# First forward stage on sums and differences of mirrored rows, in 32x32 tiles of TensorE

## The chip, the cores and the metric

The kernel runs on one core of one Trainium2 chip. A core has five engines that run side by side and wait for each other by semaphores: TensorE (PE in the profile; PEld is its loading of weights), VectorE (DVE), ScalarE (ACT), GpSimd (POOL) and SyncE (SP), which here only issues DMA transfers. Matmuls write to PSUM, eight banks of 128 partitions by 512 fp32; VectorE or ScalarE carry ("evict") the results to SBUF. The metric is the device time of one execution in microseconds, the median of three runs.

## The reference

```python
X = np.fft.rfft(x, axis=1)                      # x: 8 x 3008 x 256
Y = X * (filt_r + 1j * filt_i)[None]            # filter of 1505 x 256
y = np.fft.irfft(Y, n=3008, axis=1)
h = y.reshape(24064, 256) @ w_in                # 256 x 2048
g = 0.5 * h * (1.0 + erf(h / sqrt(2)))
out = g @ w_out                                 # 2048 x 256
```

Each of 8 batches is mixed along its 3008 rows by a Fourier transform, a filter and the transform back. Then comes a feed-forward layer with a GELU over all 24064 rows.

## The kernel before

The transform is factored as 3008 = 47 x 64. Row n of a batch is n = 64 * n1 + n2. **Stage 1** transforms over the 47 values of n1 for each n2; as x is real, frequencies k = 0..23 are enough, a real part (a sum of x times cosines) and an imaginary part (times sines), 48 rows in all. Its result R1 goes through DRAM, to be read back in another order (**r1**). **Stage 2** transforms over n2 and multiplies by the filter, **stage 3** goes back over n2, and its result R2 also goes through DRAM (**r2**); **stage 4** goes back over n1 and writes a ring `y_sb`. The feed-forward layer works on tiles of 512 rows: `mm1` makes 128 of the 2048 hidden columns, ScalarE applies the GELU, `mm2` multiplies by `w_out`.

Batch 0 is mixed first, in a form of its own (functions c1 to c4). The main loop then goes through slots, sixteen to a tile. In each slot are one step of `mm1` for tile t and one of `mm2` for tile t-1. The stages of batches 1 to 7 are spread over these slots, ahead of the tiles that need them.

```python
    for b in range(1, B):
        hi = first(b)                 # first slot that needs batch b
        if b == 1:
            s1, n1, r1, s2, n2, r2, s4, n4 = 0, 4, 15, 25, 2.8, 61, 68, 0.72
        else:
            s1, n1, r1, s2, n2, r2, s4, n4 = hi - 94, 3.5, hi - 80, hi - 69, 3.5, hi - 24, hi - 17, 1
        for u in range(16):
            put(s4 + int(u * n4), m.s4, b, u // 2, u % 2)
        for c in range(4):
            put(s1 + int(c * n1), m.s1, b, c)
            put(r1, m.r1, b, c)
            put(r2, m.r2, b, c)
        # ... s2, s3, and the loads of the next batch's x, behind gates on s2's results
    for s in range((NT + 1) * 16):
        t, jc = s // 16, s % 16
        for f, a in at.pop(s, ()):
            f(*a)
        if t >= 1:
            m.mm2(t - 1, jc)
        if t < NT:
            m.mm1(t, jc)
```

In the first sixteen slots there is no tile t-1, so only `mm1` and its GELU run there, beside stage 1 of batch 1.

Stage 1 works on four chunks of 16 columns of n2 (8 in each half). `x_sb` holds the 47 rows of n1 on 94 or, from batch 1 on, 111 of 128 partitions: columns n2 < 32 from partition 0, the others from partition 64. One matmul multiplies 47 rows by a 47x48 matrix, padded to 64 columns, on a quarter of TensorE's array:

```python
    def s1(self, b, c):
        # ...
        a = self.pa.tile([128, 2, 4, 256], BF16, tag="a", name="a_sb")
        x = self.st[b, "x"]
        ps = [[self.bank("ps_s1", "h" if i == h == 0 else "f") for h in range(2)] for i in range(2)]
        for i in range(2):
            for r in range(2):
                for h in range(2):
                    w = 8 * c + 4 * r + 2 * i
                    nc.tensor.matmul(ps[i][h][64 * r:64 * r + 64, :], lhsT=self.T1s[64 * h:64 * h + NA],
                                     rhs=x[64 * h:64 * h + NA, w:w + 2, :], start=True, stop=True)
        for i in range(2):
            for h in range(2):
                self._evac(a[:, h, 2 * i:2 * i + 2, :].rearrange("p a b -> p (a b)"), ps[i][h], False)
        o = self.st[b, "R1"].rearrange("n q c -> q n c")
        for r in range(2):
            for h in range(2):
                w = HB * h + 8 * c + 4 * r
                nc.sync.dma_start(out=o[:, w:w + 4, :], in_=a[64 * r:64 * r + 48, h])
```

`_evac(..., False)` is a copy on VectorE, `"act"` one on ScalarE. In PSUM three banks belong to tag `h` (used by `mm1` too), two to `o` (`mm2`) and three to `f`.

Before the main loop GpSimd makes the matrix and issues the loads of batch 1, eight transfers of 47 rows, and then those of `w_out`:

```python
    m.table_1_tiles(g)
    m.load_x(1)
    m.load_w_out(0)
    m.load_w_out(8)
    m.weights_4(g)
```

Of the kernel before, what the change touches and what calls it, by code (L numbers as in the profile page):

```python
# [10 lines left out]
ALU = mybir.AluOpType  # L11
FP32 = mybir.dt.float32
BF16 = mybir.dt.bfloat16
I32 = mybir.dt.int32
# [3 lines left out]
NA, NB = 47, 64  # L18
K1 = 24
HB = 32  # L20
# [9 lines left out]
class _Mix:  # L30
    def __init__(self, ctx, tc, x, filt_r, filt_i, w_in, w_out, out):
        self.tc, self.nc = tc, tc.nc
        self.x, self.filt_r, self.filt_i = x, filt_r, filt_i
        self.w_in, self.w_out, self.out = w_in, w_out, out
        self.B, self.S, self.D = x.shape
        self.DFF = w_in.shape[1]
        assert self.S == NA * NB and self.D == 256 and self.DFF == 2048
        pool = lambda name, bufs, **kw: ctx.enter_context(tc.tile_pool(name=name, bufs=bufs, **kw))
        P = bass.MemoryType.PSUM
        self.const = pool("const", 1)  # L40
        self.px = pool("px", 2)
        self.pa = pool("pa", 3)
        self.pb = pool("pb", 4)
        self.pp = pool("pp", 4)
        self.pv = pool("pv", 3)
        self.pd = pool("pd", 4)
        self.pool = pool
        self.po = pool("po", 3)
        self.py = pool("py", 1)
        self.pg = pool("pg", 2)  # L50
        self.small = pool("small", 1)
        self.dram = pool("dram", 2, space=bass.MemoryType.DRAM)
        c = self.const
# [21 lines left out]
    def load_x(self, b, lo=0, n=32, hs=(0, 1)):  # L75
        nc = self.nc
        if lo == 0 and 0 in hs:
            self.st[b, "x"] = self.px.tile([128 if b else 2 * NA, HB, 256], BF16, tag="x", name="x_sb")
        xt, o = self.st[b, "x"], 64 if b else NA
        xv = self.x[b].rearrange("(n1 h w) d -> h n1 w d", h=2, w=HB)  # L80
        for w in range(lo, lo + n, 8):
            for h in hs:
                nc.gpsimd.dma_start(out=xt[h * o:h * o + NA, w:w + 8, :], in_=xv[h][:, w:w + 8, :])  # L83

    def load_filters(self, k0, k):

        nc, D = self.nc, self.D
        for t, src in enumerate((self.filt_r, self.filt_i)):
            direct = _dram(src, k0 * D, [[NA * D, 32], [D, k], [1, D]])
            mirror = _dram(src, (NA - k0) * D, [[NA * D, 32], [-D, k], [1, D]])  # L90
            for q, a in enumerate((direct, mirror)):
                nc.gpsimd.dma_start(out=self.F[32 * q:32 * q + 32, t, k0:k0 + k, :], in_=a)
# [11 lines left out]
    def load_next(self, b, p, c, h):  # L104

        self.gate(self.st[b, "p", p][0:1, 0:1])
        self.load_x(b + 1, 8 * c, 8, (h,))

    def load_w_in(self):
        wi = self.w_in.rearrange("(dc p) j -> p dc j", p=128)  # L110
# [14 lines left out]
    def table_1(self, g):  # L125

        nc, ts = self.nc, self.nc.vector.tensor_scalar
        col = lambda name: g.tile([128, 1], FP32, name=name)
        off = g.tile([128, 2, K1], FP32, name="off")
# [12 lines left out]
        nc.vector.tensor_tensor(out=w, in0=w, in1=r, op=ALU.subtract)  # L142
        for q, s in enumerate((hc, hs)):
            nc.scalar.activation(out=self.T1[:, 48 * q:48 * q + 48], in_=w[0:2 * NA].rearrange("p a b -> p (a b)"),
                                 func=AF.Sin, scale=s[0:2 * NA])
# [131 lines left out]
            self.nc.vector.tensor_scalar(out=out, in0=in_, scalar1=scale, scalar2=None, op0=ALU.mult)  # L277


    def table_1_tiles(self, g):  # L280

        v = self.nc.gpsimd
        self.T1s = g.tile([128, 64], BF16, name="T1s")
        v.memset(self.T1s, 0.0)
        for r in (0, 64):
            v.tensor_copy(out=self.T1s[r:r + NA, 0:48], in_=self.T1[0:NA, 0:48])

    def s1(self, b, c):

        nc = self.nc  # L290
        if c == 0:
            self.st[b, "R1"] = self.dram.tile([NB, 48, 256], BF16, tag="R1", name="R1")
        a = self.pa.tile([128, 2, 4, 256], BF16, tag="a", name="a_sb")
        x = self.st[b, "x"]
        ps = [[self.bank("ps_s1", "h" if i == h == 0 else "f") for h in range(2)] for i in range(2)]
        for i in range(2):
            for r in range(2):
                for h in range(2):
                    w = 8 * c + 4 * r + 2 * i
                    nc.tensor.matmul(ps[i][h][64 * r:64 * r + 64, :], lhsT=self.T1s[64 * h:64 * h + NA],  # L300
                                     rhs=x[64 * h:64 * h + NA, w:w + 2, :], start=True, stop=True)
        for i in range(2):
            for h in range(2):
                self._evac(a[:, h, 2 * i:2 * i + 2, :].rearrange("p a b -> p (a b)"), ps[i][h], False)
        o = self.st[b, "R1"].rearrange("n q c -> q n c")
        for r in range(2):
            for h in range(2):
                w = HB * h + 8 * c + 4 * r
                nc.sync.dma_start(out=o[:, w:w + 4, :], in_=a[64 * r:64 * r + 48, h])

    def r1(self, b, c):
        bt = self.pb.tile([128, 6, 256], BF16, tag="b", name="b_sb")
# [219 lines left out]
def kernel(  # L532
# [9 lines left out]
    m = _Mix(ctx, tc, x, filt_r, filt_i, moe_w_in, moe_w_out, out)  # L542
    nc, B, S = tc.nc, m.B, m.S
# [89 lines left out]
    m.warm_up(2)  # L633
    m.T1p = g.tile([2 * NA, 2, K1, 2], BF16, name="T1p")
    nc.gpsimd.tensor_copy(out=m.T1p, in_=m.T1.rearrange("p (h r k) -> p h k r", h=2, r=2))
    m.table_1_tiles(g)
    m.load_x(1)
    m.load_w_out(0)
    m.load_w_out(8)
    m.weights_4(g)  # L640

    warm = g.tile([128, 1], FP32, name="warm")
# [12 lines left out]
    def put(slot, f, *a):  # L655
        at.setdefault(slot, []).append((f, a))

    def first(b):
        return (b * S // TCH) * 16

    for b in range(1, B):
        hi = first(b)
        if b == 1:
            s1, n1, r1, s2, n2, r2, s4, n4 = 0, 4, 15, 25, 2.8, 61, 68, 0.72
        else:
            s1, n1, r1, s2, n2, r2, s4, n4 = hi - 94, 3.5, hi - 80, hi - 69, 3.5, hi - 24, hi - 17, 1
# [9 lines left out]
        if b + 1 < B:  # L676
            for i in range(8):
                put(s2 + int(n2 * (i + 2)), m.load_next, b, i + 2, i // 2, i % 2)
# [41 lines left out]
```

## Time and profile before

The time is 772.04 us, the median of three runs between 771.49 and 772.39. The profiled execution took 771.8.

| Item (page of the profile) | Count | Mean ns | Busy us |
|---|---|---|---|
| stage 1 matmuls, 512 columns (L300) | 224 | 389 | 18.3 |
| their evictions on VectorE (L275, a_sb) | 112 | 683 | 69.5 |
| output evictions on VectorE (L519, ost) | 93 | 687 | 63.9 |
| GELU on ScalarE (L489) | 752 | 597 | 437.9 |
| mm1 matmuls (L486) | 1600 | 366 | 445.9 |
| mm2 matmuls (L513) | 2992 | 273 | 447.7 |

The profile is of one execution. A line of its groups has the line of the kernel, the engine, the operation, what it writes and reads with the shapes, the count; after the first bar the busy time in microseconds and the mean of one in nanoseconds, after the second the idle time of the engine just before, and what ended it. Busy times are unions: matmuls overlap in the array, so their means say more of latency than of cost, and the cost of a stage on TensorE is better read from when it and its neighbours start. The chain of waits goes back from the last instruction, at each step to what released it. A line of the timeline has the start and the length in microseconds, the engine, the line and the operation.

### The profile page before, as it was taken

The numbers are of one execution on the slowest core, as the hardware profiler recorded it, in microseconds if no ns is written. First come the engines' busy times: TensorE is split into PE (matmuls) and PEld (weight loads), VectorE is DVE, ScalarE is ACT, GpSimd is POOL, SyncE is SP. The second block draws the span as 40 slices with busy tenths as digits, with TensorE's granted clock in tenths as the row PEclk, the third lists the DMA queues.
The fourth block names the chain that finished last, engine by engine and source line by source line (L and its number), as shares of the span: only waits on it lengthen the run. The fifth ranks groups of instructions, "written<-read, shape, count | busy, mean of one in ns | idle before, by whom it ended". The sixth has DMA issues, their size and how long they took to land.

```text
span 771.8 us, 15047 instructions
## 1 busy us (share of the span) xinstructions
PE 763.0 (99%) x6057; PEld 527.2 (68%) x6057; DVE 399.0 (52%) x735; ACT 567.8 (74%) x978; POOL 63.7 (8%) x157
## 2 busy tenths in 40 slices
PE   8999999999999999999999999999999999999998
PEld 4757675676776766667677767666776776766666
DVE  8966755464545645457463664637646366411011
ACT  7879855897568975699656996579865798666663
POOL 8701100010000200011000110001100000000000
PEclk9999999999999999999999999999999999999999
DMA  9795645466153661636516465355553422410111
GB/s 151 130 191 130 146 113 125 130 128 150 54 147 102 136 162 41 191 77 124 142 54 181 85 133 123 81 152 97 122 137 82 138 83 69 123 42 28 42 42 55
DMA packets 87270, 85.66 MB, mean 111 GB/s; under 512 B 6688, under 2 KB 77472, under 8 KB 87200
## 3 DMA queue, kind: packets, MB, share of 16 engines
q1 hardware_dynamic: 78816, 68.70, 31.6%
q0 software_dynamic: 8384, 16.00, 14.7%
q8 instruction: 47, 0.77, 0.4%
q14 instruction: 23, 0.19, 0.1%
HBM read 54.00 MB, written 46.66 MB: 130 GB/s over the span
## 4 chain that ended last, share of the span: by engine, by line
PE 97%; DMA 1%; DVE 1%; POOL 0%; issue 0%; SPq 0%; DVEq 0%; POOLq 0%
PE ps_o L513 42%; PE ps_h L486 42%; PE ps_s L373 2%; PE ps_s L348 2%; PE ps_s L323 2%; PE ps_s L300 2%; DMA x_sb<-in_x_dram 1%; PE ps_c L434 1%; PE ps_c3t L449 0%; PE ps_c L412 0%; DMA d_sb<-R 0%; PE ps_warm L267 0%; POOL x_sb L83 0%; PE ps_c L463 0%; DVE T3i L260 0%; PE ps_c1t L399 0%
## 5 line engine op out<-in xcount | busy, mean ns | idle before, releaser
L489 ACT ACTIVATE g_sb<-ps_h 128x512 bf16<-128x512 f32 x752 | 437.9, 597 | 182.7 <-PE ps_h L486 172.0
L513 PE MATMUL ps_o<-w_out_sb,g_sb 128*128 128x256 bf16 x2992 | 447.7, 273 | 0.0
L486 PE MATMUL ps_h<-y_sb,w_in_sb 128*128 128x512 bf16 (+3 forms) x1600 | 445.9, 366 | 0.3 <-DVE a_sb L275 0.3
L513 PEld LDWEIGHTS <-g_sb 128*128 128x128 bf16 x2992 | 283.8, 98 | 134.3 <-issue 9.9
L486 PEld LDWEIGHTS <-w_in_sb 128*128 128x128 bf16 x1600 | 154.8, 98 | 23.7 <-issue 1.3
L519 DVE COPY ost<-ps_o 128x512 f32<-128x512 f32 x93 | 63.9, 687 | 143.7 <-PE ps_o L513 143.6
L331 DVE TENSOR_TENSOR p<-ps_s,F 128x512 bf16<-128x512 f32 x84 | 58.1, 692 | 105.2 <-ACT p L330 89.1
L277 DVE TENSOR_SCALAR y_sb<-ps_s 128x376 bf16<-128x376 f32 x112 | 61.0, 548 | 80.7 <-PE ps_s L373 80.7
L275 DVE CAST a_sb<-ps_s 128x512 bf16<-128x512 f32 x112 | 69.5, 683 | 27.5 <-PE ps_s L300 26.5
L275 DVE CAST v_sb<-ps_s 128x512 bf16<-128x512 f32 x84 | 57.4, 685 | 2.9 <-PE ps_s L348 2.9
L329 ACT ACTIVATE p<-ps_s 64x512 bf16<-64x512 f32 x84 | 49.8, 593 | 2.1
L330 ACT CAST p<-ps_s 64x512 bf16<-64x512 f32 x84 | 48.5, 577 | 1.0
L373 PEld LDWEIGHTS <-d_sb 96*128 96x128 bf16 x448 | 30.8, 97 | 25.6 <-DMA d_sb<-R 0.6
L102 POOL COPY gate<-p 1x1 bf16<-1x1 bf16 x48 | 8.5, 176 | 469.0 <-DVE p L333 469.0
L333 DVE TENSOR_TENSOR p<-p 128x512 bf16<-128x512 bf16 x84 | 35.7, 425 | 2.9
L373 PE MATMUL ps_s<-T,d_sb 96*128 96x94 bf16 x448 | 36.3, 204 | 0.1
L332 DVE TENSOR_TENSOR p<-p,F 128x512 bf16<-128x512 bf16 x84 | 34.9, 416 | 0.0
L83 POOL DMA_DIRECT2D x_sb<-in_x_dram x64 | 32.9, 516 | 13.3 <-issue 12.2
L323 PE MATMUL ps_s<-b_sb,T 128*128 128x256 bf16 x168 | 32.1, 273 | 0.0
L348 PE MATMUL ps_s<-p,T 128*128 128x256 bf16 x168 | 32.1, 273 | 0.0
L348 PEld LDWEIGHTS <-T 128*128 128x128 bf16 x168 | 16.4, 98 | 19.8 <-DVE p L333 0.4
L323 PEld LDWEIGHTS <-T 128*128 128x128 bf16 x168 | 16.4, 98 | 13.4
(114 smaller groups left out, 196.1 us busy)
## 6 DMA issues: line engine op xcount, KB each, us to landing
out_dram<-ost SPq DMA_DIRECT2D x93, 256.0 KB, 2.5
x_sb<-in_x_dram POOLq DMA_DIRECT2D x64, 188.0 KB, 3.8
R<-a_sb SPq DMA_DIRECT2D x112, 96.0 KB, 2.1
b_sb<-R SPq DMA_DIRECT2D x28, 384.0 KB, 4.2
R<-v_sb SPq DMA_DIRECT2D x42, 256.0 KB, 3.5
d_sb<-R SPq DMA_DIRECT2D x56, 192.0 KB, 4.9
w_in_sb<-in_moe_w_in_dram POOLq DMA_DIRECT2D x2, 512.0 KB, 10.6
w_out_sb<-in_moe_w_out_dram POOLq DMA_DIRECT2D x2, 512.0 KB, 11.9
```

The lines of the kernel that those rows point to most:

```text
L275: self.nc.vector.tensor_copy(out=out, in_=in_)
L277: self.nc.vector.tensor_scalar(out=out, in0=in_, scalar1=scale, scalar2=None, op0=ALU.mult)
L323: nc.tensor.matmul(ps[:, 256 * i:256 * i + 256], lhsT=self.T2[:, k].rearrange("p a b -> p (a b)"), rhs=self.st[b, "b", k // 6][:, k % 6, : ...
L329: nc.scalar.activation(out=p2[0:64], in_=ps[64:128], func=AF.Copy, scale=-1.0)
L330: nc.scalar.copy(out=p2[64:128], in_=ps[0:64])
L331: nc.vector.tensor_tensor(out=p1, in0=ps, in1=f(0), op=ALU.mult)
L348: nc.tensor.matmul(ps[:, 256 * i:256 * i + 256], lhsT=self.T3[:, k].rearrange("p a b -> p (a b)"), rhs=w[:, 256 * i:256 * i + 256], start= ...
L373: nc.tensor.matmul(ps[:, 94 * i:94 * i + 94], lhsT=d[:, (grp % 2) * 4 + i, 128 * half:128 * half + 128], rhs=t4, start=True, stop=True)
L486: nc.tensor.matmul(ps[:, o:o + n], lhsT=self.w_in_sb[:, dc, jc * 128:jc * 128 + 128], rhs=self.ring[:, dc, off:off + n], start=(dc == 0), ...
L489: nc.scalar.activation(out=self.st["g", t][:, jc, :], in_=ps, func=AF.Gelu)
L513: nc.tensor.matmul(ps[:, tile_i % 2, :], lhsT=g[:, jc, tile_i * 128:tile_i * 128 + 128], rhs=self.w_out_sb[:, jc, :], start=(jc == 0), sto ...
L519: nc.vector.tensor_copy(out=ost, in_=ps)
```

## The change

The 47 rows of n1 pair up: row m and row 47-m have the same cosine and opposite sines. So the real part needs only the 24 sums x[m] + x[47-m], and the imaginary part only the differences, each times a 24x24 matrix instead of a 47x48. (Row 0 is its own partner: it is added to itself, and its matrix row is halved.) The change makes sums and differences on VectorE ("fold"), a batch ahead for three of four chunks, and puts the small matrices on all sixteen 32x32 tiles of the array. It is for TensorE, which should stream half as many columns for stage 1. `[...]` marks cuts.

```diff
+        self.pf = pool("pf", 3)
-        self.pv = pool("pv", 3)
+        self.pv = pool("pv", 2)
-        self.po = pool("po", 3)
+        self.po = pool("po", 2)
[...]
+    def load_pairs(self, b, c):
+        if c == 0:
+            self.st[b, "x"] = self.px.tile([128, 2, 4, 1024], BF16, tag="x", name="x_sb")
+        t = self.st[b, "x"]
+        rows = self.x.rearrange("b (n e) d -> (b n) (e d)", e=4)
+        for i in range(2):
+            self.nc.gpsimd.indirect_dma_start(
+                out=t[:, i, c], out_offset=None, in_=rows, element_offset=(b * self.S // 4 + c) * 1024,
+                in_offset=bass.IndirectOffsetOnAxis(ap=self.rows_at[i], axis=0))
[...]
+    def load_next(self, b, p, c):
         self.gate(self.st[b, "p", p][0:1, 0:1])
-        self.load_x(b + 1, 8 * c, 8, (h,))
+        self.load_pairs(b + 2, c)
+    def load_second(self, c):
+        self.gate(self.st[1, "b", c][0:1, 0, 0:1])
+        self.load_pairs(2, c)
[...]
+    def row_indices(self, g):              # twelve iotas: rows m and 47-m, in four groups of 32 partitions
[...]
+    def table_1_pairs(self, g):            # on GpSimd: the 0/1 matrix "pick" that selects rows of T1
[...]
+    def table_1_rows(self):
+        ps = self.bank("ps_t1", "n")
+        self.nc.tensor.matmul(ps[:, 0:48], lhsT=self.pick[0:2 * NA], rhs=self.T1[:, 0:48], start=True, stop=True)
+        self._evac(self.T1s[:, :, 0:K1], ps[:, 0:48].rearrange("p (r k) -> p r k", r=2), "act")
+
+    def fold(self, b, c):
+        x = self.st[b, "x"]
+        s = self.st[b, "fold", c] = self.pf.tile([128, 4, 256], BF16, tag="xs", name="xs")
+        d, m, s = x[:, 0, c], x[:, 1, c], s.rearrange("p a b -> p (a b)")
+        self.nc.vector.tensor_tensor(out=s, in0=d, in1=m, op=ALU.add)
+        self.nc.vector.tensor_tensor(out=d, in0=d, in1=m, op=ALU.subtract)
 
     def s1(self, b, c):
[...]
+        rows = (self.st.pop((b, "fold", c)), self.st[b, "x"][:, 0, c].rearrange("p (a b) -> p a b", a=4))
+        ps = [self.bank("ps_s1", "f" if g else "h") for g in range(4)]
+        for j in range(2):
             for r in range(2):
-                for h in range(2):
-                    w = 8 * c + 4 * r + 2 * i
-                    nc.tensor.matmul(ps[i][h][64 * r:64 * r + 64, :], lhsT=self.T1s[64 * h:64 * h + NA],
-                                     rhs=x[64 * h:64 * h + NA, w:w + 2, :], start=True, stop=True)
+                for g in range(4):
+                    o, w, k = 64 * j + 32 * r, 2 * j, slice(32 * g, 32 * g + K1)
+                    nc.tensor.matmul(ps[g][o:o + 32, :], lhsT=self.T1s[k, r, :],
+                                     rhs=rows[r][k, w:w + 2, :].rearrange("p a b -> p (a b)"), start=True, stop=True)
+        for g in range(4):
+            self._evac(a[:, g].rearrange("p a b -> p (a b)"), ps[g], "act" if g == 3 or b == 1 and g == 1 else False)
+        o = self.st[b, "R1"].rearrange("(g w) (r k) c -> r w k g c", g=4, r=2)
+        for j in range(2):
+            for r in range(2):
+                for i in range(2):
+                    p = 64 * j + 32 * r
+                    nc.sync.dma_start(out=o[r, 4 * c + 2 * j + i], in_=a[p:p + K1, :, i])
[...]
-    m.table_1_tiles(g)
-    m.load_x(1)
+    m.row_indices(g)
+    m.load_pairs(1, 0)
+    m.table_1_pairs(g)
+    m.table_1_rows()
+    m.load_pairs(1, 1)
     m.load_w_out(0)
     m.load_w_out(8)
+    for i in (2, 3):
+        m.load_pairs(1, i)
[...]
-            s1, n1, r1, s2, n2, r2, s4, n4 = 0, 4, 15, 25, 2.8, 61, 68, 0.72
+            s1, n1, r1, s2, n2, r2, s4, n4 = 1, 3.5, 15, 26, 2.8, 62, 69, 0.7
[...]
+            f = (0, 3, 7, 10) if b == 1 else (62, 64, 66) if b == 2 else [first(b - 1) - 79 + 3 * i for i in range(3)]
+            put(f[c] if c < len(f) else s1 + 2, m.fold, b, c)
[...]
+            if b == 1:
+                put(r1 + 1, m.load_second, c)
```

A chunk is now four groups of four columns of n2, each group on its own 32 partitions (24 in use). Each of four PSUM banks takes one group. The rows are gathered by index, 128 rows of 1024 numbers to a transfer, since mirrored rows run backwards. `x_sb` is loaded two batches ahead.

More of the change, by code (lines that the diff above doesn't have):

```diff
@@ L77, in load_x @@
         if lo == 0 and 0 in hs:
-            self.st[b, "x"] = self.px.tile([128 if b else 2 * NA, HB, 256], BF16, tag="x", name="x_sb")
-        xt, o = self.st[b, "x"], 64 if b else NA
+            self.st[b, "x"] = self.px.tile([2 * NA, HB, 256], BF16, tag="x", name="x_sb")
+        xt, o = self.st[b, "x"], NA
         xv = self.x[b].rearrange("(n1 h w) d -> h n1 w d", h=2, w=HB)
@@ L102, in gate @@
         self.nc.gpsimd.tensor_copy(out=g, in_=t)
-    def load_next(self, b, p, c, h):
+    def load_next(self, b, p, c):
         self.gate(self.st[b, "p", p][0:1, 0:1])
-        self.load_x(b + 1, 8 * c, 8, (h,))
+        self.load_pairs(b + 2, c)
+    def load_second(self, c):
+        self.gate(self.st[1, "b", c][0:1, 0, 0:1])
+        self.load_pairs(2, c)
     def load_w_in(self):
@@ L128, in table_1 @@
         col = lambda name: g.tile([128, 1], FP32, name=name)
-        off = g.tile([128, 2, K1], FP32, name="off")
+        self.off = off = g.tile([128, 2, K1], FP32, name="off")
         nc.vector.memset(off[:, 0, :], 0.25)
@@ L277, in _evac @@
             self.nc.vector.tensor_scalar(out=out, in0=in_, scalar1=scale, scalar2=None, op0=ALU.mult)
-    def table_1_tiles(self, g):
-        v = self.nc.gpsimd
-        self.T1s = g.tile([128, 64], BF16, name="T1s")
-        v.memset(self.T1s, 0.0)
-        for r in (0, 64):
-            v.tensor_copy(out=self.T1s[r:r + NA, 0:48], in_=self.T1[0:NA, 0:48])
+    def row_indices(self, g):
+        self.rows_at = [g.tile([128, 1], I32, name=n) for n in ("rows_d", "rows_m")]
+        for t, base, cm in zip(self.rows_at, (0, 16 * NA), (16, -16)):
+            for q in range(4):
+                self.nc.gpsimd.iota(t[32 * q:32 * q + 32], pattern=[[0, 1]], base=base + 4 * q, channel_multiplier=cm)
+        for q in range(4):
+            self.nc.gpsimd.iota(t[32 * q:32 * q + 1], pattern=[[0, 1]], base=4 * q, channel_multiplier=0)
+    def table_1_pairs(self, g):
+        v = self.nc.gpsimd
+        cols = self.iota(g, "cols32", [128, 128], [[0, 4], [1, 32]])
+        half, pick = g.tile([128, 1], FP32, name="half0"), g.tile([128, 128], BF16, name="pick")
+        v.memset(half, 1.0)
+        v.memset(half[0:1], 0.5)
+        v.tensor_scalar(out=pick, in0=cols, scalar1=self.p, scalar2=half, op0=ALU.is_equal, op1=ALU.mult)
+        self.T1s = g.tile([128, 2, 32], BF16, name="T1s")
+        v.memset(self.T1s, 0.0)
+        self.pick = pick
+    def table_1_rows(self):
[8 more added lines that the diff above has]
+        self.nc.vector.tensor_tensor(out=d, in0=d, in1=m, op=ALU.subtract)
     def s1(self, b, c):
@@ L292, in s1 @@
             self.st[b, "R1"] = self.dram.tile([NB, 48, 256], BF16, tag="R1", name="R1")
[L293 to L296, printed above, removed]
+        a = self.pa.tile([128, 4, 2, 256], BF16, tag="a", name="a_sb")
+        rows = (self.st.pop((b, "fold", c)), self.st[b, "x"][:, 0, c].rearrange("p (a b) -> p a b", a=4))
+        ps = [self.bank("ps_s1", "f" if g else "h") for g in range(4)]
+        for j in range(2):
             for r in range(2):
-                for h in range(2):
-                    w = 8 * c + 4 * r + 2 * i
-                    nc.tensor.matmul(ps[i][h][64 * r:64 * r + 64, :], lhsT=self.T1s[64 * h:64 * h + NA],
-                                     rhs=x[64 * h:64 * h + NA, w:w + 2, :], start=True, stop=True)
[L302 to L309, printed above, removed]
+                for g in range(4):
[10 more added lines that the diff above has]
+                    nc.sync.dma_start(out=o[r, 4 * c + 2 * j + i], in_=a[p:p + K1, :, i])
     def r1(self, b, c):
@@ L675 @@
             put(s2 + int(n2 * p) + 4, m.s3, b, p)
-        if b + 1 < B:
-            for i in range(8):
-                put(s2 + int(n2 * (i + 2)), m.load_next, b, i + 2, i // 2, i % 2)
+        if b + 2 < B:
+            for i in range(4):
+                put(s2 + int(n2 * (2 * i + 3)), m.load_next, b, 2 * i + 3, i)
     put(20, m.table_4, m.T4, m.T1p, m.wt, "f", "act")
```

## The prediction

> **What bounds the kernel now.** I read the busy shares and the clock row first, then the chain of waits by line, then the groups of instructions, and then two stretches of the timeline: one in the steady part and the start of the main loop.
>
> ```profile
> PE 763.0 (99%) x6057; PEld 527.2 (68%) x6057; DVE 399.0 (52%) x735; ACT 567.8 (74%) x978; POOL 63.7 (8%) x157
> ...
> PEclk9999999999999999999999999999999999999999
> ...
> PE 97%; DMA 1%; DVE 1%; POOL 0%; issue 0%; SPq 0%; DVEq 0%; POOLq 0%
> ```
>
> TensorE is busy 763 of 771.8 us at full clock and is 97% of the chain. So a microsecond taken from TensorE's stream is a microsecond of the kernel, and everything that the change adds elsewhere is free as long as TensorE never waits for it. VectorE, at 52%, has room on average.
>
> ```profile
> L275 DVE CAST a_sb<-ps_s 128x512 bf16<-128x512 f32 x112 | 69.5, 683 | 27.5 <-PE ps_s L300 26.5
> L330 ACT CAST p<-ps_s 64x512 bf16<-64x512 f32 x84 | 48.5, 577 | 1.0
> L333 DVE TENSOR_TENSOR p<-p 128x512 bf16<-128x512 bf16 x84 | 35.7, 425 | 2.9
> R<-a_sb SPq DMA_DIRECT2D x112, 96.0 KB, 2.1
> ```
>
> These are the durations I use: 0.683 us for one eviction on VectorE, some 0.6 on ScalarE, 0.425 for a bf16 add of 512 columns, 2.1 us for a store of the first stage to land. Now the stage itself, in TensorE's timeline:
>
> ```profile
> 209.52 0.60 PE L486 MATMUL ps_h<-y_sb,w_in_sb 128*128 128x384 bf16 x4
> 210.05 0.63 PE L300 MATMUL ps_s<-x_sb,T1s 47*64 47x512 bf16 x8
> 210.61 0.61 PE L513 MATMUL ps_o<-w_out_sb,g_sb 128*128 128x256 bf16 x4
> 211.06 0.60 PE L486 MATMUL ps_h<-y_sb,w_in_sb 128*128 128x384 bf16 x4
> 211.50 0.27 PE L513 MATMUL ps_o<-w_out_sb,g_sb 128*128 128x256 bf16 x1
> ```
>
> The columns are start, length, engine and line. From the first feed-forward group to the output group that follows it, 211.06 to 211.50, is 0.44 us. With a first-stage block between them (209.52 to 210.61) it is 1.09. So one block costs 0.65 us, and 28 of them 18 us: 2.4% of the kernel, all that the change can work on. In the trace the eight matmuls start in two volleys: four at 210.054, .057, .061 and .064, four at 210.294 to .303. The next matmul starts 0.32 us after the second volley.
>
> The start of the main loop is the one place where TensorE is not comfortably the bound:
>
> ```profile
> 39.66 0.63 PE L300 MATMUL ps_s<-x_sb,T1s 47*64 47x512 bf16 x8
> 40.12 4.88 DVE L275 CAST a_sb<-ps_s 128x512 bf16<-128x512 f32 x8
> ...
> 48.79 2.48 DVE L275 CAST a_sb<-ps_s 128x512 bf16<-128x512 f32 x4 [1.03 <-PE ps_h L486]
> ```
>
> Blocks of batch 1 start at 39.7, 42.0, 44.8 and 47.2, one every 2.5 us, because the first 16 slots have only the first half of the feed-forward in them. VectorE is busy 10.3 of the 14.3 us from 39.7 to 54.0 already.
>
> **What the Trainium skill says.** (1) "TensorE: Matmul & The Clock Gate", Part 3, gives the length of packed tiles as one matmul plus about 4 ns for each further tile, up to 16 tiles of 32x32. The trace agrees: the four tiles of a volley start 3 to 4 ns apart. (2) "TensorEngine Tiling (Array Packing)", PSUM Bottleneck: tiling speeds up TensorE but not the evacuation, so both ScalarE and VectorE should do it. The trace can show only half: four evictions take 2.48 us after a block of 0.65. (3) "VectorE: DVE Perf Modes", the tier table: a bf16 tensor_tensor from SBUF runs at two elements a cycle. The trace fits: 512 columns take 425 ns, and the one-column form (the row of 128x1 f32) takes 160, so 0.52 ns a column. (4) "DMA: Bandwidth & Descriptors", Rules for kernel authors, asks to coalesce small transfers, which mostly pay overhead. The change goes the other way, and the trace shows the price of an issue: eight loads of d_sb in a row occupy the queue for 3.60 us, 0.45 each.
>
> **The change part by part.**
>
> *Matmuls (saves).* Eight matmuls in two volleys become sixteen in one. Removed: the 0.24 us between the volleys. Added: twelve more pairs before the last start, at 3.4 ns, 0.04 us. I take 0.18 us a block, the lower side of 0.20. In batches 2 to 7 that is 24 x 0.18 = 4.3 us. The turns into and out of the small tiles stay, so 0.47 of 0.65 us remains.
>
> *Folds (added on VectorE).* Two adds of 128x1024 a chunk, each 160 + 1024 x 0.52 = 690 ns: 1.4 us a chunk, 39 us for 28 chunks. For batches 2 to 7 three of the four lie in the gap after the previous batch's first stage or in an idle stretch; the fourth stands between the evictions of blocks 0 and 1. VectorE then has 3 x 0.683 + at most 1.4 = 3.4 us per block against a spacing of about 3.5. Free for TensorE.
>
> *Eviction.* One of four goes to ScalarE (+0.6 us a block on an engine at 74%, with 0.4 us free per slot of about 1 us). Free.
>
> *Stores to R1.* Four of 96 KB become eight of 48 KB a block. At 0.45 us each this is 3.6 us of SyncE a block, as much as the spacing of blocks (3.5), plus 0.4 us for each output store. In batch 4 today the blocks start at 304.1, the last R1 store is issued at 318.6, and the reads of b_sb start at 320.9, +16.8 from the first block; one lands 3.4 us later; the second stage needs it at +24.3. With a full queue the last of 32 stores goes out at about +17.6, lands at +20, the read at +23.4. Stage two is due at 24.3 - 0.7 = +23.6. So it just fits in the mean; batch 3, whose read is issued at +18.0 today, misses by about one. I book 0.2 x 6 = 1.2 us.
>
> *Loads.* A batch becomes four pairs of gathers of 128 rows of 1024, 2.1 MB landed instead of 1.5, because 32 rows are read where 24 count. Batches 2 to 7 load a batch earlier than needed: hidden.
>
> *The start (loses).* (a) The new small matrix is made on GpSimd behind two gathers, and a matmul on TensorE waits for it before the last part of batch 0. GpSimd is free at 29.4 (today's T1p ends there); twelve iotas at 0.13 make 31.0, two gathers at an estimated 1.0 each (a plain load of 47 rows takes 0.5, one of w_out 0.9) 33.0, and five small operations 33.9. TensorE comes by at 32.9: +1.0. (b) Each chunk of batch 1 is now a chain on one engine: fold 1.4, matmuls 0.5, two evictions 1.4, some 0.1 in handovers, 3.4 us. VectorE ends batch 0 at 40.2 today, so at 41.2; the fourth block starts at 41.2 + 3 x 3.4 + 1.4 = 52.8 instead of 47.2. (c) Chunks 2 and 3 are queued behind w_out. From 31 to 46 that queue moves 2.55 MB, 0.17 MB/us; now it has 3.15 MB, with the third chunk landing at about 49 and the last at 52, where the chain would want them at 48.0 and 51.4: +1.0. (d) After the fourth block ScalarE has two evictions and two GELUs before the last bank of slot 15 is free, 2.3 us, then two matmul groups: 3.2 us, so the second half begins at 53.8 + 3.2 = 57.0 instead of 50.4. Loss: 6.6 us.
>
> *Sum.* 6.6 + 1.2 - 4.3 = +3.5 us: 772.0 becomes 775.5.
>
> **The rivals.** (A) *The pure gain.* The folds of batch 1 hide better than I think, gathers are as cheap as plain loads, the queue keeps up. Then the start loses 3 and the rest gains 5: 770. For it: the evictions of batch 1 were split evenly between the engines, and the slots look tuned. Against it: a chain of 3.4 us against a spacing of 2.5 has no slack to hide in. (B) *The store queue becomes a bound.* Each of six batches waits some 1.5 us before stage two: 775.5 + 8 = 783. For it: 3.6 us of issue for 3.5 us of spacing. Against it: the landings may be quicker at half the size. (C) *Sixteen tiles do not run together*, being held up by loading 16 sets of weights: no gain in TensorE, 780. For it: in today's trace no block has more than four tiles at once. Against it: the four pairs start within 12 ns.
>
> **Range and chances.** The start can lie between +4 and +10, the matmuls between -5 and 0, the queue between 0 and +8; they hardly go together at their ends. Predicted 775.5, 8 times in 10 between 770.5 and 783. A gain of 2% would need 15.4 us of a stage that costs 18: 1 in 100. A loss of 2% needs a long start together with B: 3 in 100. Within 2%: 96.
>
> **What would show it.** The block in the timeline should read 0.45 to 0.50 us with one volley. The fold should be 0.69 us. R1 stores on SyncE should stand back to back, with the reads of b_sb at about +20 from the first block, and perhaps idle time of TensorE before stage two. The chain of waits should show VectorE's folds, and gathers, between 40 and 57 us, with the first output matmuls at about 57. I am wrong if these start by 53, if the fold takes over 1 us, or if a wait for x shows in later batches.

## The result and the profile after

The changed kernel takes 785.28 us, the median of four runs (784.99 to 786.97), against 772.21 for the kernel before: ratio 1.017, interval 1.0156 to 1.0185. It is slower, and outside the predicted range of 770.5 to 783.0. The profiled execution took 783.3 us, against 771.8. The table further down divides these 11.5 us; the medians lie 13.1 apart.

The page after, in the parts that the prediction showed of before:

```profile
PE 762.2 (97%) x6282; PEld 529.0 (68%) x6282; DVE 414.3 (53%) x759; ACT 585.5 (75%) x1011; POOL 87.8 (11%) x147
...
PEclk9999999999999999999999999999999999999999
...
PE 90%; DMA 5%; DVE 2%; ACT 1%; POOL 1%; issue 1%; SPq 0%; DVEq 0%; POOLq 0%; ACTq 0%
...
L292 DVE CAST a_sb<-ps_s 128x512 bf16<-128x512 f32 x80 | 50.3, 683 | 27.3 <-PE ps_s L343 19.1
...
R<-a_sb SPq DMA_DIRECT2D x224, 48.0 KB
```

TensorE is busy for nearly the same time (762 us against 763), but no longer 99% of the time: transfers now hold 5% of the chain of waits instead of 1%. VectorE lost 32 evictions (112 to 80) and the stores of stage 1 doubled, as written. A table of three stretches shows where TensorE stands idle. The columns are the stretch, its length, busy time (and instructions) of TensorE, its weight loading, VectorE, ScalarE and GpSimd, then TensorE's granted clock, the busy share of the 16 DMA engines and GB/s. First the kernel before:

```profile
30.00:60.00 30.00, 29.46 (x298) 18.77 (x296) 19.08 (x31) 24.18 (x50) 6.48 (x14) 1.00 0.93 190
60.00:130.00 70.00, 69.89 (x553) 47.41 (x552) 47.73 (x88) 52.88 (x92) 5.63 (x16) 1.00 0.54 120
130.00:760.00 630.00, 630.00 (x4860) 436.73 (x4859) 303.29 (x546) 466.87 (x799) 27.26 (x80) 1.00 0.43 106
```

and the kernel after:

```profile
30.00:60.00 30.00, 22.07 (x250) 13.41 (x248) 17.95 (x29) 21.07 (x47) 12.76 (x21) 0.94 0.86 140
60.00:130.00 70.00, 65.31 (x497) 45.16 (x496) 41.65 (x78) 51.24 (x89) 16.94 (x24) 0.98 0.73 163
130.00:760.00 630.00, 629.48 (x5092) 437.58 (x5091) 325.22 (x580) 480.58 (x825) 33.30 (x48) 1.00 0.43 109
```

TensorE idles 7.9 us at the start, where it idled 0.5, and 4.7 us during batch 1, where it idled 0.1. After that it stands still for 0.5 us of 630, and it is there that the change pays. The budget can be read from when TensorE starts the output matmuls (`mm2`) of a tile:

| Stretch | before | after | difference | predicted |
|---|---|---|---|---|
| span start to first `mm2` | 50.40 | 58.86 | +8.46 | +6.6 |
| to `mm2` of tile 4 (batch 1's stages 2 to 4) | 63.85 | 70.22 | +6.37 | 0 |
| to `mm2` of tile 46, the last (batches 2 to 7) | 647.41 | 643.65 | -3.76 | -3.1 |
| to the end | 10.07 | 10.53 | +0.46 | 0 |

The steady part went as predicted. A block of stage 1 in the timeline of the kernel after:

```profile
317.53 0.59 PE L529 MATMUL ps_h<-y_sb,w_in_sb 128*128 128x512 bf16 x2
...
318.06 0.39 PE L343 MATMUL ps_s<-xs,T1s 24*32 24x512 bf16 x4
318.07 0.40 PE L343 MATMUL ps_s<-x_sb,T1s 24*32 24x512 bf16 x4
318.09 0.39 PE L343 MATMUL ps_s<-xs,T1s 24*32 24x512 bf16 x4
318.10 0.40 PE L343 MATMUL ps_s<-x_sb,T1s 24*32 24x512 bf16 x4
...
318.43 0.61 PE L556 MATMUL ps_o<-w_out_sb,g_sb 128*128 128x256 bf16 x4
```

From 317.53 to 318.43 is 0.90 us; less the 0.44 without a block, a block costs 0.46 where it cost 0.65. The losses are in the first two rows of the table. This is what VectorE and TensorE waited for between 60 and 130 us (engine, line, what it waited for: total, times, longest):

```profile
DVE v_sb L292 <- DMA R<-v_sb: 3.8, 1, 3.8
...
PE ps_s L366 <- DVE v_sb L292: 2.7, 1, 2.7
...
PE ps_s L416 <- DMA d_sb<-R: 1.0, 1, 1.0
PE ps_s L366 <- DMA b_sb<-R: 1.0, 1, 1.0
```

A store of `v_sb`, issued at 78.45, landed at 90.10, after 11.64 us. The first line is from the chain of waits after (start, length, what), the second from the page of before (count, size, median us to landing):

```profile
78.45 11.64 DMA R<-v_sb
...
R<-v_sb SPq DMA_DIRECT2D x42, 256.0 KB, 3.5
```

The eviction that wanted its buffer waited, and TensorE behind it. Around it, sixteen gathers for batches 2 and 3 were issued between 69.5 and 105 us. This stall lies between the `mm2` of tile 1 and that of tile 2, which are 20.5 us apart (before 16.5): 4.0 of the 6.4 us. Of the rest, 1.1 us lie between tiles 0 and 1, where TensorE waits for a read of R1 (`b_sb`) that is issued at 65.5 us, before the first of these gathers (before: at 54.5, so it slid by 2.5 us more than the start). And 1.2 lie between tiles 2 and 4, with a wait for `d_sb`, whose reads are issued from 112.8 us on, after the last gather.

### The profile page after: what moved, and what is told of

It is laid out like the page before. It is cut to its first block, busy times and chain, and to the rows that moved or that the text cites. A ratio compares the mean times of both kernels' runs of the same rounds, so it can differ in the third digit from the quotient of the medians.

```text
span 783.3 us, 15725 instructions
## 1 busy us (share of the span) xinstructions
PE 762.2 (97%) x6282; PEld 529.0 (68%) x6282; DVE 414.3 (53%) x759; ACT 585.5 (75%) x1011; POOL 87.8 (11%) x147
## 2 busy tenths in 40 slices
DMA packets 92649, 89.60 MB, mean 114 GB/s; under 512 B 7528, under 2 KB 78312, under 8 KB 92576
## 4 chain that ended last, share of the span: by engine, by line
PE 90%; DMA 5%; DVE 2%; ACT 1%; POOL 1%; issue 1%; SPq 0%; DVEq 0%; POOLq 0%; ACTq 0%
PE ps_o L556 40%; PE ps_h L529 39%; PE ps_s L416 2%; PE ps_s L366 2%; PE ps_s L391 2%; DMA R<-v_sb 2%; PE ps_s L343 1%; DMA R<-a_sb 1%; DMA b_sb<-R 1%; DMA x_sb<-in_x_dram 1%; PE ps_c L477 1%; PE ps_c3t L492 1%; DMA d_sb<-R 0%; PE ps_c L455 0%; ACT g_sb L532 0%
## 5 line engine op out<-in xcount | busy, mean ns | idle before, releaser
L292 DVE CAST a_sb<-ps_s 128x512 bf16<-128x512 f32 x80 | 50.3, 683 | 27.3 <-PE ps_s L343 19.1
L114 POOL COPY gate<-p 1x1 bf16<-1x1 bf16 x20 | 3.6, 179 | 334.9 <-DVE p L376 334.9
L391 PEld LDWEIGHTS <-T 128*128 128x128 bf16 x168 | 16.5, 99 | 20.3 <-DVE p L376 0.7
L93 POOL DMA_INDIRECT x_sb<-in_x_dram,rows_d x28 | 27.2, 972 | 12.0 <-issue 8.4
```

What stands on the lines that cost most here:

```text
L292: self.nc.vector.tensor_copy(out=out, in_=in_)
L391: nc.tensor.matmul(ps[:, 256 * i:256 * i + 256], lhsT=self.T3[:, k].rearrange("p a b -> p (a b)"), rhs=w[:, 256 * i:256 * i + 256], start= ...
```

## Experiments

Each run was timed beside the kernel before on its chip. "First `mm2`", "tile 4" and "tile 46" are starts as in the table. My theory was that the 6.4 us came from early loads meeting transfers that are waited for, and that the start lost by its wait for the small matrix and the chain over VectorE. The rivals were the buffers that the change took away, the form of the loads (gathers), and for the start the amount of data to move.

### The start: the wait for the small matrix

In the changed kernel TensorE waits 3.04 us for GpSimd before it makes the small matrix (start, length, engine, line, operation; in brackets the idle time before it, and what ended it):

```profile
34.53 0.20 PE L320 MATMUL ps_t<-T,pick 94*128 94x48 bf16 x1 [3.04 <-POOL pick L313]
```

```diff
+    m.table_1_pairs(g)         # before the loads; the matmul after table_3(1)
-    m.table_1_pairs(g)
-    m.table_1_rows()
```

> The changed kernel, with the 0/1 matrix made on GpSimd before its filter copies, and the small matrix multiplied and evicted before the second half of batch 0, so that nothing of it stands between batch 0's last two parts. If the late matrix and the table load behind it are a loss of their own, the first mm1 moves from 44.0 back to about 40.3 us and the time falls by 3.0 to 3.8, to about 781.7. Rival: the start is paced by the folds and by the landing of the gathers, which come at the same times, so the earlier matrix only moves the wait into the chunks: under 1 us.

785.53 us, first `mm2` at 58.74: no gain. The matmul now stood so early that TensorE waited 4.3 us for it there instead. The second run loads ScalarE's GELU table earlier:

```diff
+    nc.scalar.activation(out=warm, in_=m.p, func=AF.Gelu)   # ahead of the index tables
```

> The changed kernel, with only ScalarE's dummy GELU (and so its table load of 1.28 us) put before the eviction of the small matrix. If the table load is pushed behind that eviction and then delays the evictions of batch 0's last part, the time falls by 1.3 to 1.6, to about 783.8. Rival: TensorE is held by the matrix alone, and the table load hides: 0.

784.72 us (ratio 1.016, 1.0126 to 1.0194), first `mm2` at 59.34. Executions between 782.1 and 787.2 can't tell 1.3 us from nothing, but the trace can: TensorE still waits 3.5 us for the matrix, and the first `mm1` stands at 44.22 (43.97 in the changed kernel). So the table isn't what holds it.

### Batch 1: a third buffer, or fewer loads at once

```diff
-        self.pv = pool("pv", 2)
+        self.pv = pool("pv", 3)      # room made by smaller constants
```

> The changed kernel with three v_sb buffers as before instead of two (room made by a smaller block of ones for the warm-up matmuls and by putting two index tables into a buffer of stage 1); the gathers stay as they are. If the missing buffer alone makes the stall in stage 3 of batch 1, the first v_sb stores still land late or not, but TensorE no longer waits: 2.7 to 4 us less, about 782. If the gathers' congestion is the cause, the store of v_sb still takes some 11 us to land and part of the stall stays or comes back later: under 2.5 us.

787.02 us. From tile 1 to tile 2 it took 20.7 us, as in the changed kernel (20.5; before 16.5), but for another reason: `v_sb` waited for no store any more, and ScalarE stood 3.7 us with a late signal, as described below. This moved the next evictions of `v_sb` back too (80.2, then 86.96), which gave the store its time. So it isn't shown that the third buffer took the wait away, and what it is worth is left open. The other run kept two buffers and moved the loads:

```diff
-                put(r1 + 1, m.load_second, c)                 # 8 gathers in a row
+                put(s2 + int(n2 * (2 * i + 3)), m.load_second, 2 * i + 3, i)
+                put(s4 + 1 + 3 * i, m.load_third, i)          # was where load_second is now
```

> The changed kernel with batch 2's gathers spread over stage 2 of batch 1 (one pair of gathers every 5 or 6 slots), and batch 3's during stage 4 of batch 1; two v_sb buffers. If eight gathers in a row, and eight more soon after, starve the stores, the v_sb stores land in 3 to 5 us instead of 11.6, the wait for them vanishes with two buffers too, and the time falls by 4 to 6, to about 780. If the buffer count is the cause, the stall stays: within 1 us of the changed kernel.

782.02 us (ratio 1.0118, 1.0101 to 1.0135). From tile 1 to tile 2 it takes 16.3 us, and no wait for `R<-v_sb` is left between 76 and 94 us, with two buffers. From the first `mm2` to tile 4 it is 66.42 us. Four executions whose gathers stand as in the changed kernel (its own, the first two runs, and its repeat below) took 70.2, 70.4, 68.1 and 68.0 us for that, and 19.1 to 20.5 from tile 1 to tile 2. So the loads close together made the store late, and two buffers did not cover it. The first `mm2`, at 59.07, did not move.

### The start once more, and the folds

```diff
 # on top of the spaced gathers: the small matrix before the first gathers,
+            if q == 4:
+                m.table_1_rows()                              # its matmul late in batch 0
```

> e4 with the small matrix made early on GpSimd and its one matmul placed late in batch 0's stage loop, where it is ready. The last kernel with an early matrix put that matmul so early that TensorE waited there instead. If a wait of 3 us at this place, and the halved clock after it, cost the start 3.7 us, the first mm1 comes at 40.3 to 41 instead of 44 to 45, no window in the first 45 us shows a clock under 0.95 at that place, and the time falls from 782.0 to about 778.5. Rival: the gathers' landing and the folds set the pace anyway: 781 to 782.

789.30 us, on another chip than the run before it; the first `mm2` is still at 59.12. 7 us are lost between 111 and 123 us, to late signals of the kind described below. The next run leaves out the folds of batch 1 (its sums are then those of the plain rows):

```diff
+            if b > 1:
                 put(f[c] if c < len(f) else s1 + 2, m.fold, b, c)
```

> e5 without the folds of batch 1 (stage 1 of batch 1 takes the mirrored rows as they are in place of sums and differences, so its result is left out): everything else, gathers included, stays. If the chain fold, matmul, eviction on VectorE sets the pace of the first 16 slots, they shorten by 3 to 4 us against e5 (about 775). If the landing of the last two pairs of gathers behind w_out sets it, the third and fourth block start when these land, at most 1.5 us sooner: 777 to 778.

787.97 us, first `mm2` at 58.15: 1 us for eight folds.

### The start undone

```diff
 # batch 1 in the form of the kernel before, with its plain loads and slots; pairs from batch 2 on
+            put(s1 + int(c * n1), m.s1 if b > 1 else m.s1_old, b, c)
```

> e4's spread gathers, but batch 1 as before the change: 64-wide tiles, plain loads, no folds, the old slots; pairs from batch 2 on. The matrix is multiplied in slot 22. If the losses all lie in the start and in batch 1, and the gain of 0.19 us a block holds in batches 2 to 7, the time is before minus 4.5 plus up to 1 for waits of stage 2 and 0.5 for the output buffers at the end: 768.5 to 769.5, faster than both. Rival: gathers and doubled stores cost the later batches too: 771 or more.

778.16 us. First `mm2` at 50.25, tile 3 at 97.24: the kernel before, within 0.2 us. But tile 4 came at 121.45 instead of 114.25. ScalarE's timeline there:

```profile
103.99 0.60 ACT L568 ACTIVATE g_sb<-ps_h 128x512 bf16<-128x512 f32 x1 [0.82 <-PE ps_s L452]
108.35 0.60 ACT L568 ACTIVATE g_sb<-ps_h 128x512 bf16<-128x512 f32 x1 [3.77 <-PE ps_s L452]
112.63 0.60 ACT L568 ACTIVATE g_sb<-ps_h 128x512 bf16<-128x512 f32 x1 [3.68 <-PE ps_h L565]
```

ScalarE stood idle for 3.8 and 3.7 us with its matmuls long started. TensorE's completion signals reach the others at 103.97, 105.44, 106.89, 108.33 and 109.77, one every 1.44 us, while GpSimd issues eight gathers in a row (101.1 to 111.0). Six more come in a heap at 112.6 to 112.9, after the last gather. Such heaps stand in the third-buffer run and the two runs of the section before too; all four ran on one chip. I took it for the cost of gathers in a row, and tested that.

### Where the loads of batch 3 stand, and their form

```diff
-                    put(s4 + 1 + 3 * i, m.load_third, i)
+                    put(first(2) - 93 + int(3.5 * i), m.load_third, i)   # after each block of batch 2
```

> Batch 1 in its old form with its old loads, pairs from batch 2 on, the gathers of batch 2 spaced over the second stage of batch 1 (one pair every 5 us), and those of batch 3 moved from the eight-in-a-row during the fourth stage of batch 1 to one pair after each first-stage block of batch 2. If the 7 us lost at 101 to 113 us in the run with the old start come from eight gathers in a row, they are gone: 768.5 us (767 to 770), tile 4 starts its output matmuls at 114.3, and TensorE has no idle stretch over 1.3 us after 25 us. If they come from something else in the changed memory layout or in the new form itself (a rival), the time stays at 777 to 778. A third theory, that gathers are dear wherever they stand, puts a new stall at 125 to 145 us: 772 to 778.

777.32 us. From tile 3 to tile 4 it takes 16.9 us again, as before, but tile 6 is at 152.05 (before 145.34), and between 139 and 148 us TensorE waited for the reads of batch 2's R1:

```profile
PE ps_s L402 <- DMA b_sb<-R: 4.1, 1, 4.1
```

The gathers (119.8 to 133.8) met the first-stage stores, whose last issue slid to 140.4. After the wait, from 144 to 148 us, TensorE's granted clock was 0.63. With the third output buffer:

> The same with the third output buffer that the kernel before had (room made by smaller constants). The last output copies then don't wait for a store, some 0.5 us at the end: 768.0 us if that is all, within 0.3 us of the run with two buffers if the wait lies beside the last matmuls anyway.

776.45 us, the same stall (tile 6 at 151.79). The form was tested on the changed kernel, with a plain transfer for each gather; it leaves out the reversal of the mirrored rows:

```diff
-            self.nc.gpsimd.indirect_dma_start(out=t[:, i, c], [...] in_=rows, in_offset=[...])
+            self.nc.gpsimd.dma_start(out=t[:, i, c], in_=[...])   # 4 x 32 rows of 1024
```

> The changed kernel with a plain transfer of the same 128 rows of 4 KB in the place of each gather, at the same places in the program; the reversal of the mirrored rows is left out, so the output is that of another sum. If the gathers' form [...]causes the late start and the late store of v_sb, both shrink: store of v_sb back at 4 us, 778 to 780 us. If the bytes in a row cause it (rival), nothing changes: 785 us, v_sb's store still lands after 10 us or more.

796.88 us, slower by 10.6 than the repeat below on the same chip: first `mm2` at 64.68. (A row has 2 KB, not the 4 of the expectation.) Not a clean test, because these transfers brought 21,500 packets under 512 bytes of their own (29,032 in all, 7,528 in the changed kernel). So the gathers' form is neither blamed nor cleared.

> The changed kernel once more beside these three on the same chip, as their measure: 785 us (784 to 787) if the loss in batch 1 belongs to the program; more, with idle stretches of all engines during gathers, if how much a row of gathers costs depends on the chip or on what else its memory does.

786.32 us, and `v_sb` waited 3.4 us for its store again: the loss in batch 1 belongs to the program. Here the first `mm2` came at 61.06 and tile 4 68.02 us later, so single executions of one program differ by some 2 us in each of these rows.

```diff
-                    put(s4 + 1 + 3 * i, m.load_third, i)
+                    put(73 + 3 * i, m.load_third, 73 + 3 * i, i)   # behind a GELU of the slot before
```

> Old start, three output buffers, and the gathers of batch 3 put where the transfers of the kernel before left a gap: one pair every 3 slots from slot 73, after the reads of d_sb and before the first-stage stores of batch 2. If all that the early loads cost is that they meet stores and reads that are waited for, both stalls (101 to 113 us with the old start, 141 to 146 us with gathers between the stores of batch 2) are gone and only the steady gain of 0.75 us in each of six batches remains: 768.0 us (767 to 769.5), tile 4 at 114.3 and tile 6 at 145.3 less at most 1. If the six batches' gain is bought with any placement of the extra transfers (rival), another stall of 4 us or more shows up and it is 774 or more.

771.51 us (ratio 0.9989, 0.9979 to 0.9999), with the third output buffer. Of the stall 1.7 us are left (tile 5 to tile 6 takes 16.2 us, before 14.6): the last gathers (to 119.7) overlap the first stores, which begin at 118.4. And the run with the old start unchanged, on another chip:

> The run with the old start and eight gathers in a row at 101 to 111 us once more, unchanged. If the stall of 7 us there belongs to the program: 778 us and tile 4 at 121.4. If it comes and goes with the chip it runs on: about 770, tile 4 at 114 to 115.

769.36 us (ratio 0.9957, 0.9943 to 0.9970), 8.8 us less than the same kernel took on the first chip. The stretch from 103 to 114 us, in the first run and then in the repeat:

```profile
103.00:114.00 11.00, 7.02 (x58) 4.55 (x57) 4.20 (x8) 2.74 (x6) 6.62 (x10) 0.83 1.09 219
```

```profile
103.00:114.00 11.00, 10.90 (x114) 8.14 (x114) 7.80 (x15) 5.92 (x11) 6.94 (x10) 1.00 1.09 234
```

DMA engines and GpSimd are as busy, but TensorE works 10.9 us of 11. So the program alone doesn't make the stalls with late signals, and my theory of gathers in a row fell; their cause stays open. Where the gathers of batch 3 end at 111 us, tile 4 to tile 46 takes 642.8 us; where they end at 119.7 it takes 644.5, and at 133.8 648.6 and 649.5. So they cost nothing, 1.7 or some 6 us. It is a question of what they meet.

### The start, on a chip without late signals

The edit of the fifth run, with the loads of batch 3 from slot 73:

> The start of the change, with its small matrix made before the first gathers and multiplied late in batch 0, the gathers of batch 2 spaced, and those of batch 3 in the gap from slot 73. If the wait for the matrix is a loss of its own: 3 us below the run with spaced gathers alone (782.0), and 0.8 more for tile 4: 778.2. If the chain fold, matmul, eviction and the late rows set the pace and the wait only hid behind them (rival): first output matmul at 58.5 or later, 781.5.

783.84 us. From the first `mm2` to tile 4 it takes 64.51 us, 0.7 more than before: with the spaced gathers of batch 2 and the later ones of batch 3, batch 1 loses almost nothing, though the start is the change's own. The first `mm1` comes at 39.72 (44 in the changed kernel), yet the first `mm2` at 60.55. The waits from 40 to 61 us:

```profile
DVE xs L334 <- DMA x_sb<-in_x_dram,rows_m: 6.1, 2, 5.4
PE ps_s L349 <- DVE xs L334: 5.8, 2, 4.4
```

The third chunk's rows, queued behind `w_out`, arrive at 52. The granted clock is lower here too (columns as in the table of stretches; the third number from the end is TensorE's granted clock):

```profile
45.00:50.00 5.00, 3.40 (x20) 0.93 (x8) 1.29 (x2) 3.26 (x6) 0.17 (x1) 0.66 1.25 210
50.00:55.00 5.00, 2.09 (x19) 0.60 (x20) 2.16 (x4) 0.74 (x2) 0.00 (x0) 0.75 0.85 182
55.00:60.00 5.00, 4.64 (x28) 1.65 (x28) 3.09 (x5) 4.21 (x9) 0.00 (x0) 0.56 0.56 112
```

In the kernel before it is 1.00 in all of these. Five `mm1` matmuls that took 1.47 us at 41.31 took 2.31 at 54.10. In the changed kernel the clock was 0.66 from 35 to 40 us, after the wait for the matrix. What of the start's loss is the clock is not shown. Without the folds of batch 1 (left out again):

> The same without the eight adds of batch 1 (left out: the matmuls take the rows as loaded, so batch 1 is wrong in the output). If the folds on VectorE are the pace of the start: first output matmul at 53 to 54 (5 us earlier). If the rows' arrival or ScalarE is: within 1.5 us of the run with folds.

782.18 us, first `mm2` at 57.80, and a wait of 5.9 us for the same rows. Then the rows first:

```diff
+    for i in (1, 2, 3):
+        m.load_pairs(1, i)
     m.load_w_out(0)
     m.load_w_out(8)
```

> The run with the new start and an early matrix, with all four pairs of gathers of batch 1 issued before w_out. If the pace of that start is set by the third chunk's rows waiting behind w_out (TensorE idle for 5.0 us before the third block, at 47.8 to 52.8 us), the wait goes: third block at 47.5, fourth at 51, first output matmul at 55 instead of 60.5, about 778.5 us. If the bandwidth is what lacks (rival), w_out itself comes late: first output matmul at 58 or later and a wait for w_out.

783.37 us, first `mm2` at 58.09. The blocks now stand at 40.6, 43.7, 47.0 and 50.0, but the last evictions wait for the stores of an earlier block:

```profile
DVE a_sb L298 <- DMA R<-a_sb: 4.2, 1, 4.2
PE ps_h L535 <- DVE a_sb L298: 3.5, 1, 3.5
```

> The same without the adds of batch 1 (left out, so that batch 1 is wrong in the output). With the rows early, the folds' own share of the start shows: if the chain fold, matmul, eviction of 3.4 us a block is what is left, the blocks stand 2.5 us apart without it, the first output matmul is 3 to 4 us earlier than with folds (51 to 52), and the time 775. If rows or w_out still set the pace: within 1 us of the run with folds.

781.42 us, again without the folds: blocks at 40.0, 42.2, 45.2 and 47.6, and the same wait, longer (6.2 us). First `mm2` at 56.42. In each order of the transfers something else was waited for. With the rows first the DMA share is 1.06 to 1.29 in the three stretches of 5 us from 40 to 55 us (packet times are summed, so it can pass 1); before it was 1.39, 0.95 and 0.54. Packets of x take 12.9 us of all 16 engines there, against 9.1 before.

### A version that beats both

Old start, spaced gathers of batch 2, those of batch 3 between the last read of `d_sb` and the stores of batch 2, three output buffers:

> The fastest version so far (batch 1 in its old form, pairs from batch 2 on, gathers of batch 2 spaced and those of batch 3 in a row from 101 us) with the third output buffer of the kernel before. The last output copies don't wait: 0.5 us off the end, 768.9 us against some 772.5 before, ratio 0.995; 778 if the stall at 101 to 111 us is met again.

769.08 us, ratio 0.9949 (0.9935 to 0.9963): faster than before. Its table:

```profile
30.00:60.00 30.00, 28.62 (x279) 18.00 (x278) 17.89 (x30) 23.79 (x51) 8.22 (x29) 1.00 0.95 200
60.00:130.00 70.00, 69.89 (x590) 47.84 (x589) 50.89 (x94) 55.42 (x97) 16.99 (x24) 1.00 0.73 154
130.00:760.00 630.00, 630.00 (x5055) 439.98 (x5053) 316.29 (x567) 478.32 (x821) 33.44 (x48) 1.00 0.43 107
```

Batch 1 has the DMA share of the changed kernel (0.73) and none of its idle time. Tile 4 to tile 46 takes 642.81 us, 4.60 less than before, and from tile 46 to the end 10.05 instead of the 10.55 that two output buffers gave with the same start.

## Why the prediction was wrong

**Bound.** Right for the steady part only. In batch 1 TensorE came to wait for transfers, which I had weighed only as queues of issues. At the start it waited for folds and evictions that waited for transfers themselves.

**Matmuls.** Right: 0.19 us a block instead of 0.18, and sixteen starts within 0.05 us (318.059 to 318.109), 3.3 ns apart. That bears out the Trainium skill, "TensorE: Matmul & The Clock Gate", Part 3, for sixteen tiles, which the trace of before could not show; rival C is out. From tile 4 to tile 46 the gain is 4.6 us where stage 2 doesn't wait, in the last run, against 4.3 predicted.

**Folds and evictions.** Right: the two halves of a fold took 0.68 and 0.69 us, and with the old start TensorE doesn't stand still between 130 and 760 us, so neither shows from batch 2 on.

```profile
43.74 0.68 DVE L328 TENSOR_TENSOR xs<-x_sb 128x1024 bf16<-128x1024 bf16 x1
...
44.45 0.69 DVE L329 TENSOR_TENSOR x_sb<-x_sb 128x1024 bf16<-128x1024 bf16 x1
```

**Stores to R1.** About right: of the 4.6 us the changed kernel kept 3.76, so 0.8 came back, where I booked 1.2. The reads of `b_sb` go out 20.9 us (batch 3) and 19.1 us (batch 4) after the first block, near the predicted 20. Rival B did not happen. In batch 1, for which I booked nothing, TensorE waited 1.0 us for the read of R1.

**Loads: "Batches 2 to 7 load a batch earlier than needed: hidden."** This step failed. I asked when the data are needed and not what else the engines carry while they move. The Trainium skill, "DMA: Bandwidth & Descriptors", Queues, rings and completion order, says that each DMA engine takes turns between the queues that have work, packet by packet, so a store shares its engines with every gather in flight. The trace fits: 11.64 us for a store that took 3.5. The stall behind that store cost 4.0 of the 6.4 us (2.6 to 4.0 in four executions of the same batch 1). With the gathers of batches 2 and 3 spaced it was gone (tile 1 to tile 2 in 16.3 us), and once the gathers of batch 3 came later too, the whole row took 64.5 us with the change's own start. In the last run, with the old start, it takes 63.9 (before 63.85). With only their place changed, the loads of batch 3 cost 0, 1.7 or some 6 us. The two `v_sb` buffers did not cover a store of 11.64 us, and were enough once the gathers were spaced. The rest of the 6.4 us, 1.0 of it the late read of R1 and 1.0 the wait for `d_sb`, has no cause shown.

**The start.** Right in sign, 8.5 instead of 6.6, with its terms mis-sized. Step (a): TensorE came by at 31.5, not 32.9, and waited 3.0 us, with the matrix behind two gathers of 1.07 and 0.97 us and 0.82 for its own making, where I had booked 1.0. But without that wait nothing was won. Step (b), the chain of 3.4 us a block, was near: 3.1, 3.7 and 3.7. Leaving out the folds brought the first `mm2` forward by 1.0, 2.8 and 1.7 us in three pairs of runs. Step (c), "chunks 2 and 3 are queued behind w_out: +1.0", sized as the delay of one queue, is where the runs point. The changed kernel needs 3.8 us more of all DMA engines there, and each order of the transfers made a different one late, by 3.5 to 5.9 us of TensorE's time. That fits, but no run separates it from three others: the stores of R1, doubled in number (the last is issued at 63.7 us, before 52.2, and with the rows first SyncE waited 7.3 us for its own earlier ones), the evictions moved to ScalarE, and the clock of 0.5 to 0.75 after TensorE's waits. The old start undoes all of them together, and brings the loss back (first `mm2` at 49.6 to 51.1).

**The end.** The two output buffers cost 0.5 us, which I had left out.

What stays open: what a third `v_sb` buffer alone would save; why the plain transfers landed later than gathers of the same bytes; and how the start's loss divides between the bytes of x, the small stores of R1, the evictions on ScalarE and the clock, since no run changed one of them alone.

## What to carry to other kernels

Data that are needed late still use the DMA engines now: put a prefetch where the transfers that someone waits for are few, and look at the DMA share of that stretch, not of the span. Judge a cheaper inner loop by its startup too, where it has no earlier batch to hide its preparation under; a hybrid (old form once, new form after) may be the better kernel. And when taking away one wait only moves it to another engine, look for the resource that all of them share.

## What the runs showed that I had not expected

One kernel, unchanged, took 778.16 us on one chip and 769.36 on another, while the kernel before took 773.13 and 772.76 there. On the first chip TensorE's signals came once in 1.44 us during eight gathers in a row, and the clock granted in the stretch from 103 to 114 us fell to 0.83. Runs on three other chips don't show this. So a stall seen on a single chip should be repeated on another before it counts.
